# Gate's copy of the logits and its tanh issued one place later, with the steps behind them, in all batches but the last

## The chip, the cores and the metric

The kernel runs on one core of a Trainium2 chip. The metric is the time of one execution on the device, in microseconds. The core's engines are TensorE (PE, with its weight loads shown apart as PEld), VectorE (DVE), ScalarE (ACT), GpSimd (POOL) and SyncE (SP, which here only issues DMAs). Each works through its own instructions in order and waits where an operand or a buffer is not there yet.

## What is computed

Attention with a capped score, then a mixture of experts with one expert per token. The sizes are 8 batches, 12 heads, 448 tokens, head width 64; 3584 tokens of width 768 go to 8 experts of inner width 1024, each of which keeps at most 80 tokens.

```python
scores = cap * np.tanh(np.matmul(q, k.transpose(0, 1, 3, 2)) / sqrt(64) / cap)
attn = softmax(scores)                       # over the last axis
x = (attn @ v).transpose(0, 2, 1, 3).reshape(3584, 768)
logits = x @ w_gate
expert_idx = np.argmax(logits, axis=1)
gate_w = softmax(logits)[np.arange(N), expert_idx]
# per expert: of its tokens the `capacity` ones with the largest gate_w
out[tok_idx] = gate_w[tok_idx, None] * (relu(x[tok_idx] @ w1[e]) @ w2[e])
```

## The kernel before

**Attention.** Two heads make a step `t`, 48 in all, six per batch. `qk` (L1019, L1026) multiplies keys by queries into a PSUM tile `sc` (two buffers), and ScalarE writes tanh of it to `e` (L1027). `expo` (L1032) takes the exp in place. `av` (L1043) multiplies `e` by the values. The softmax sums go POOL (`esum`, L1051 and L1053, into `t`), VectorE (`erem`, L1061, up to step 33), TensorE (`sums`, `sp`, L1068 and L1070), VectorE (`st`, `rc`, `r`). `scaled` (L1085) and `turned` (L1093) make `x` and its transpose `xb`.

**Order.** The order of everything is written out by hand; the instructions stand on each engine as the Python issues them. An even step runs `q0 q1 y m a0 a1 b q2 q3 s b x a2 a3 r b u`, an odd one `q0 q1 y a0 a1 b q2 q3 u n b x a2 a3 b`. Here q is qk with its tanh, x and y the two halves of the exp, a is av, s and r the two erem of the even step, u the sums (odd steps), n and m scaled and turned. Each `b` is a place: three in a step, numbered 0 to 2 in the text. At a place `background` issues work from three lists: `urgent` (the gate), `low` (gathers for the first experts) and `bg` (ranks of tokens, and the expert order). An entry is (cost in ns, function, gap): it is issued only if at least `gap` places have passed since the last entry of its list, and while the place's quota lasts. The quota is the cost still listed, shared out over the places left in the batch, at least 600 and at most 2200 (3000 from step 33 on); an entry may overdraw it once. From step 33 on an estimate of VectorE's backlog holds entries back as well.

**The gate** of a batch is put on `urgent` by `m` of the step in which the batch's last `x` is made (step 8 for batch 0, then every six). Its steps before: `product` multiplies `x` by the gate weights into `lgp` (twelve matmuls, L1112) and ScalarE copies the result to `lgs` (L1119); `turn` transposes it on TensorE into `lt` (L1126); `choice` on VectorE sums, takes the maximum and the differences `d` (L293 to L295), ScalarE takes tanh of half of `d` into `tau` (L296), VectorE finds the chosen expert (L297 to L301); `key` makes the sort key from `tau` (L304 to L312); `later` makes the gate weight and stores it (L317 to L322, the store on SP's queue) and puts the batch's rank steps on `bg`.

**Ranks** (L387 to L421): a row of keys is spread by TensorE (`psk`) and copied by ScalarE (`krow`), VectorE compares (`gb` of up to 896 columns, L408, and `gl`, L395), TensorE counts (`pd`, L415), VectorE adds (`dfc`, L421). Batch 4's are mixed with the steps that order the experts (`pr...`). The tiles `lgp`, `lt`, `sp`, `psk` and `pd` share two PSUM buffers.

**Experts.** Eight weight tiles are loaded ahead from step 39; after step 49 the expert products (L758) run, with what is left of the lists between them.

Of the kernel before, what the change touches and what calls it, by code (L numbers as in the profile page):

```python
# [7 lines left out]
F32 = mybir.dt.float32  # L8
# [3 lines left out]
AF = mybir.ActivationFunctionType  # L12
# [5 lines left out]
B, H, S, D = 8, 12, 448, 64  # L18
# [6 lines left out]
NC = S // C  # L25
# [4 lines left out]
E = 8  # L30
# [6 lines left out]
OB = 5  # L37
# [76 lines left out]
def attn_moe(ctx, tc, q2, k, v, cap, wg, w1, w2, capacity, ct, out):  # L114
    nc = tc.nc
# [152 lines left out]
        nc.tensor.matmul(psn[:, 0:E], ones[:C, :], hs, start=True, stop=True)  # L268
        copy(dst, psn[:, 0:E])

    def gate_math(sm, lt, b, kcb, ohb, gdst, usb=None, cmb=None, ohvb=None, queue=nc.sync):

        sh = [C, NC, E]
        lg = sm.tile(sh, F32, name=f"lg{b}", tag="lg")
        mx = sm.tile([C, NC], F32, name=f"mx{b}", tag="mx")
        d = sm.tile(sh, F32, name=f"d{b}", tag="d")
        tau = sm.tile(sh, F32, name=f"tau{b}", tag="tau")
        cand = sm.tile(sh, F32, name=f"cand{b}", tag="cand")
        cm = sm.tile([C, NC], F32, name=f"cm{b}", tag="cm") if cmb is None else cmb
        pw = sm.tile(sh, F32, name=f"pw{b}", tag="pw")  # L280
        wsc = sm.tile([C, NC], F32, name=f"wsc{b}", tag="wsc")
        rd = sm.tile(sh, F32, name=f"rd{b}", tag="rd")
        w = sm.tile(sh, F32, name=f"w{b}", tag="w")
        u = sm.tile([C, NC], F32, name=f"u{b}", tag="u")

        def up(a):
            return a.rearrange("p (c a) -> p c a", a=1).broadcast_to(sh)

        def row(key):
            return cst(key, C).rearrange("p (a e) -> p a e", a=1).broadcast_to(sh)  # L290

        def choice():
            nc.vector.tensor_reduce(lg, lt.rearrange("p c g e -> p c e g"), axis=AX.X, op=ALU.add)  # L293
            nc.vector.tensor_reduce(mx, lg, axis=AX.X, op=ALU.max)
            nc.vector.tensor_tensor(d, up(mx), lg, op=ALU.subtract)  # L295
            nc.scalar.activation(tau, d, AF.Tanh, scale=0.5)  # L296
            nc.vector.scalar_tensor_tensor(cand, d, 0.0, row("rev"), op0=ALU.is_equal, op1=ALU.mult)  # L297
            nc.vector.tensor_reduce(cm, cand, axis=AX.X, op=ALU.max)
            nc.vector.tensor_tensor(ohb, row("rev"), up(cm), op=ALU.is_equal)
            nc.vector.scalar_tensor_tensor(pw, ohb, 1.0, row("pow"), op0=ALU.mult, op1=ALU.mult)  # L300
            nc.vector.tensor_reduce(wsc, pw, axis=AX.X, op=ALU.add)  # L301

        def key():
            nc.vector.tensor_scalar(rd, tau, 1.0, 0.0, op0=ALU.add, op1=ALU.add, accum_out=dump[:C])  # L304
            nc.vector.reciprocal(rd, rd)
            nc.vector.tensor_tensor(w, tau, rd, op=ALU.mult)
            nc.vector.tensor_reduce(u, w, axis=AX.X, op=ALU.add)
            if usb is not None:
                nc.vector.tensor_scalar(usb, u, 2.0 ** -28, None, op0=ALU.max)
            nc.vector.scalar_tensor_tensor(kcb, u, 2.0 ** -28, wsc, op0=ALU.max, op1=ALU.mult)  # L310
            if ohvb is not None:
                nc.vector.tensor_tensor(ohvb, rev[:C].rearrange("p (a e) -> p a e", a=1).broadcast_to(sh), up(cm), op=ALU.is_equal)  # L312
        return choice, key, lambda: gate_weights(sm, sh, tau, rd, b, gdst, queue)

    def gate_weights(sm, sh, tau, rd, b, gdst, queue):
        w2 = sm.tile(sh, F32, name=f"w2{b}", tag="w2")
        nc.vector.scalar_tensor_tensor(w2, tau, 1.0, rd, op0=ALU.subtract, op1=ALU.mult)  # L317
        g = sm.tile([C, NC], F32, name=f"g{b}", tag="g")
        nc.vector.tensor_reduce(g, w2, axis=AX.X, op=ALU.add)
        nc.vector.tensor_scalar(g, g, -1.0, 1e-9, op0=ALU.mult, op1=ALU.add)  # L320
        nc.vector.reciprocal(g, g)
        queue.dma_start(gdst, g)  # L322
# [513 lines left out]
    def attention_rowmax(sm, pl, b):  # L836
# [55 lines left out]
            nc.tensor.transpose(lt[:, c, 0], lg[:, c * C:(c + 1) * C], cst("ident", 32)[:, :32])  # L892
        kcb = sm.tile([C, NC], F32, name="gkc", tag="gkc")
        ohb = sm.tile([C, NC, E], F32, name="goh", tag="goh")
        for f in gate_math(sm, lt[:, :, :, 0:E], "g", kcb, ohb, gdv[:, bass.ds(b * NC, NC)]):
            f()
        nc.sync.dma_start(kcd[:, bass.ds(b * NC, NC)], kcb)
        nc.sync.dma_start(ohd[:, bass.ds(b * NC, NC)], ohb)
# [63 lines left out]
    urgent = []  # L962
# [11 lines left out]
    with ExitStack() as a2:  # L974
# [139 lines left out]
        def gate(b):  # L1114
            def product():
                logits(b, range(NP))
                lp = st["lp", b]
                lg = sm.tile([96, S], F32, name=f"lgs{b}", tag="lgs", bufs=1)
                nc.scalar.copy(lg, lp[0:96, :S])  # L1119
                st["lgs", b] = lg  # L1120

            def turn():
                lg = st["lgs", b]
                lt = ps1.tile([C, NC, 3, 32], F32, name=f"lt{b}", tag="misc", bufs=2)
                for c in range(NC):
                    nc.tensor.transpose(lt[:, c].rearrange("p g e -> p (g e)"), lg[:, c * C:(c + 1) * C], cst("ident", 96)[:, :96])  # L1126
                st["lt", b] = lt

            def math():
                cs = slice(b * NC, (b + 1) * NC)  # L1130
                lt = st["lt", b][:, :, :, 0:E]
                if b < OB:
                    st["math"] = gate_math(sm, lt, b, kc[:, cs], oh[:, cs], gdv[:, cs], us[:, cs], cms[:, cs])
                else:
                    ws = slice(b * NC - OCOL, (b + 1) * NC - OCOL)
                    st["math"] = gate_math(sm, lt, b, kc[:, cs], oh[:, cs], gdv[:, cs], None, cmn[:, ws], ohv[:, ws], nc.sync if b < B - 1 else nc.gpsimd)
            def end(pd):
                r = st["rank"] = consts.tile([C, RCOL], F32, name="rank")
                nc.vector.tensor_tensor(osd, osd, dfc2, op=ALU.add)
                nc.vector.tensor_reduce(r, acc2, axis=AX.X, op=ALU.add)  # L1140
                nc.vector.tensor_tensor(r, r, osd, op=ALU.subtract)
                n = pd.shape[-1]
                nc.vector.tensor_tensor(r[:, :n], r[:, :n], pd, op=ALU.subtract)
                st["chain"]()
            def later():
                st["math"][2]()
                if b < OB:
                    steps = list(ranks(krow, gp, ps1, "misc", b, acc, dfc, 0, 0, []))
                else:
                    steps = list(ranks(krow, gp, ps1, "misc", b, acc2, dfc2, CAND, OCOL, [e * SL for e in range(E)]))  # L1150
                if b == OB - 1:
                    kept = list(prune(krow, gp, ps1, "misc"))
                    n = next(i for i, x in enumerate(kept) if x[0] == 1750)
                    steps = [steps[0], kept[0], *steps[1:4], kept[1], *steps[4:7], kept[2], *steps[7:9], *kept[3:n], *steps[9:], *kept[n:]]
                if b > OB:
                    bg.insert(0, steps.pop(0))
                bg.extend(steps)
                now[2] = now[0]
                ready_at[2] = clock[1]

            def finish():
                st["math"][2]()
                steps = list(ranks(krow, gp, ps1, "misc", b, acc2, dfc2, CAND, OCOL, [e * SL for e in range(E)], end=end))
                f0, f1, f2, f6, f3, f4, f5, f8 = final_order(sm, lambda: ps1.tile([128, 512], F32, name="pcn", tag="misc", bufs=2))
                parts = [(50, lambda i=i, h=h: stored(nc.gpsimd, b, i, slice(NB // 2 * h, NB // 2 * h + NB // 2)), 1) for i in range(4) for h in range(2)]
                head = [(400, f0, 0), steps[0], (200, f1, 1), steps[1], (200, f2, 1), steps[2], (200, f6, 1), (200, f3, 0), steps[3],
                        steps[4], (300, f4, 1), *steps[5:8], (300, f5, 1), *steps[8:10], (300, f8, 1), *steps[10:]]
                n = 4
                for x in parts:
                    head.insert(n, x)  # L1170
                    n += 2
                bg.extend(head)
            st["wait"]()
            urgent.append((300, product, 0 if b < OB else 1))
            urgent.append((300, turn, 1 if b < OB else 2))
            if b < OB - 1:
                urgent.append((2500, lambda: (math(), st["math"][0](), st["math"][1](), later()), 1))
                return
            urgent.append((1900, lambda: (math(), st["math"][0]()), 1 if b < OB else "ordered"))
            urgent.append((1900, lambda: st["math"][1](), 0))  # L1180
            urgent.append((1000, finish if b == B - 1 else later, 0))

        now = [0, -9, -9, -9]
# [240 lines left out]
```

## Time and profile before

| | us |
|---|---|
| median of 3 runs | 524.43 (523.38 to 525.9) |
| profiled execution: time | 523.92 |
| profiled execution: span, first to last instruction | 522.1 |
| TensorE busy in the span | 477.3 (91%) |
| VectorE busy | 344.2 (66%) |
| ScalarE busy | 328.6 (63%) |
| POOL busy | 257.4 (49%) |

Attention takes the span to about 400 us, the experts the rest. A busy share is a mean over both. In a row of the trace, what stands in brackets is the time for which the engine was idle just before the instruction, and who released it.

### The profile page before, as it was taken

The page shows a single profiled execution, that of the slowest core. Times are in us where ns is not written, and L with a number is a line of the kernel's source. Part 1 is how long each engine was busy: PE and PEld are TensorE (multiplying, and loading weights), DVE is VectorE, ACT ScalarE, POOL GpSimd, SP SyncE. Part 2 cuts the span into 40 slices and gives each one's busy share as a digit, 9 for nine tenths or more (in the row PEclk, how much of TensorE's full clock was granted, in tenths as well). Part 3 has the DMA queues.
Part 4 walks back from the last instruction along what each step waited for, and adds up shares of the span by engine and source line. Part 5 has one row for each costly group of instructions (what it writes and reads, how often), then busy time and mean ns, then how long its engine had stood idle before and what let it go on. Part 6 is the DMA issues. An engine that isn't in the chain of part 4 may idle for free. (4 is left out here: it accounts for less than half of the span.)

```text
span 522.1 us, 13512 instructions
## 1 busy us (share of the span) xinstructions
PE 477.3 (91%) x5476; PEld 218.7 (42%) x5476; DVE 344.2 (66%) x783; ACT 328.6 (63%) x326; POOL 257.4 (49%) x175
## 2 busy tenths in 40 slices
PE   6899999999899999999999998989999978887894
PEld 2223322332332323333323332233335778787894
DVE  1177789878988998899889866984669624512000
ACT  4998879788787978788777875857890101011111
POOL 0666657554664645576356443635964064043001
PEclk9999999999999999999999999989999998999999
DMA  6655359667765774578538769783659789999931
GB/s 165 184 167 148 92 105 222 173 187 87 199 212 131 105 231 108 94 143 251 131 87 163 166 157 257 120 216 106 196 109 315 239 220 407 381 383 398 361 127 45
DMA packets 74103, 99.03 MB, mean 190 GB/s; under 512 B 16976, under 2 KB 59248, under 8 KB 74032
## 3 DMA queue, kind: packets, MB, share of 16 engines
q1 hardware_dynamic: 72048, 93.45, 65.8%
q0 software_dynamic: 1984, 4.63, 2.8%
q8 instruction: 45, 0.74, 0.6%
q14 instruction: 26, 0.21, 0.2%
HBM read 74.54 MB, written 23.51 MB: 188 GB/s over the span
## 5 line engine op out<-in xcount | busy, mean ns | idle before, releaser
L1027 ACT ACTIVATE e<-sc,scl 128x896 f32<-128x896 f32 x168 | 162.4, 1005 | 55.0 <-PE sc L1019 53.0
L1043 PE MATMUL av<-e,vr 128*32 128x448 f32 x1536 | 174.3, 546 | 3.7 <-ACT e L1032 1.9
L1053 POOL TENSOR_TENSOR t<-t,e 128x896 f32<-128x896 f32 x48 | 109.4, 2279 | 92.6 <-ACT e L1032 85.6
L1032 ACT ACTIVATE e<-e,capt 128x1792 f32<-128x1792 f32 x96 | 153.6, 1601 | 0.0
L1019 PE MATMUL sc<-qt,kt 64*128 64x448 f32 x576 | 139.1, 585 | 12.5 <-ACT e L1027 7.5
L1051 POOL TENSOR_TENSOR t<-e 128x896 f32<-128x896 f32 x48 | 106.1, 2211 | 74.9 <-ACT e L1032 74.9
L1061 DVE SCALAR_TENSOR_TENSOR t<-t,e 64x448 f32<-64x448 f32 x68 | 93.0, 1378 | 29.7 <-ACT e L1032 28.5
L1043 PEld LDWEIGHTS av<-e,vr 128*32 128x32 f32 x1536 | 46.7, 109 | 100.8 <-issue 72.1
L1019 PEld LDWEIGHTS sc<-qt,kt 64*128 64x128 f32 x576 | 49.7, 191 | 89.8 <-issue 41.7
L408 DVE TENSOR_SCALAR_CACHE_REDUCE gb<-krow,kc 112x896 bf16<-112x896 f32 (+16 forms) x59 | 53.9, 930 | 8.0 <-ACT krow L388 4.4
L758 PE MATMUL yt<-thv,w 128*64 128x80 f32 x1152 | 44.5, 235 | 10.1 <-issue 10.1
L758 PE MATMUL hp<-xt,w 128*64 128x80 f32 x1152 | 44.7, 237 | 2.4 <-issue 2.4
L758 PEld LDWEIGHTS yt<-thv,w 128*64 128x64 f32 x1152 | 41.9, 137 | 12.0 <-issue 12.0
L758 PEld LDWEIGHTS hp<-xt,w 128*64 128x64 f32 x1152 | 42.5, 140 | 5.1 <-issue 4.8
L1073 DVE STREAM_TRANSPOSE st<-sp 128x448 f32<-128x448 f32 x24 | 15.5, 647 | 34.1 <-PE sp L1070 18.6
L802 POOL DMA_INDIRECT out_dram<-ysv,si x6 | 5.7, 956 | 56.0 <-ACT ysv L801 37.4
L1093 DVE STREAM_TRANSPOSE xb<-x 128x448 f32<-128x448 f32 x48 | 30.8, 644 | 1.6
L1068 PE MATMUL sp<-t,ones 128*32 128x448 f32 x192 | 28.2, 551 | 3.4 <-DVE t L1061 2.0
L774 ACT COPY ty0v<-yt 128x240 f32<-128x240 f32 x6 | 2.1, 358 | 46.1 <-PE yt L758 46.1
L1085 DVE TENSOR_TENSOR x<-av,r 128x448 f32<-128x448 f32 x48 | 29.5, 616 | 0.8
L1026 PE MATMUL sc<-qt,kt 64*64 64x448 f32 x192 | 23.6, 562 | 0.0
L774 DVE COPY ty1v<-yt 128x240 f32<-128x240 f32 x1 | 0.4, 408 | 33.8 <-ACT ty0v L774 33.8
(216 smaller groups left out, 302.9 us busy)
## 6 DMA issues: line engine op xcount, KB each, us to landing
w<-in_w_dram SPq DMA_DIRECT2D x36, 512.0 KB, 8.2
w<-in_w_dram SPq DMA_DIRECT2D x48, 384.0 KB, 6.0
kt<-in_k_dram SPq DMA_DIRECT2D x96, 112.0 KB, 3.6
qt<-in_q_dram SPq DMA_DIRECT2D x96, 112.0 KB, 2.8
xs<-xb SPq DMA_DIRECT2D x28, 336.0 KB, 5.9
vr<-in_v_dram SPq DMA_DIRECT2D x24, 256.0 KB, 3.6
out_dram<-zero SPq DMA_DIRECT2D x4, 1536.0 KB, 7.2
vr<-in_v_dram SPq DMA_DIRECT2D x24, 192.0 KB, 3.0
```

What stands on the lines that cost most here:

```text
L408: nc.vector.tensor_scalar(g, krow[:, x:y], kp, 0.0, op0=ALU.is_ge, op1=ALU.add, accum_out=a)
L758: nc.tensor.matmul(ps[j // per][64 * h:64 * h + 64, j % per * m:(j % per + 1) * m], w[:, 128 * j + 64 * h:128 * j + 64 * h + 64], x[:, kk, ...
L1019: nc.tensor.matmul(ps[:, h, :S], s["k"][w, x:x + CK], s["q"][w], start=True, stop=True)
L1027: nc.scalar.activation(s["e"][:, 2 * c:2 * c + 2], ps[:, :, :S], AF.Tanh, scale=scl)
L1032: nc.scalar.activation(x, x, AF.Exp, scale=capt)
L1043: nc.tensor.matmul(st["av", u, f][32 * g:32 * g + 32, :S], st[p]["v"][:, g % 2, c, 32 * f:32 * f + 32], late(p) if c == NK else st[p]["e"] ...
L1051: nc.gpsimd.tensor_tensor(t1, e[:, 0:2], e[:, 2:4], op=ALU.add)
L1053: nc.gpsimd.tensor_tensor(s["es"], s["es"], e[:, 4:6], op=ALU.add)
L1061: nc.vector.scalar_tensor_tensor(t1[w, h], t1[w, h], 0.0, late(p)[w], op0=ALU.add, op1=ALU.add)
L1068: nc.tensor.matmul(sp[32 * g:32 * g + 32, :S], ones[:, 0:32], s["es"][:, g % 2, :], start=True, stop=2 * u < RMB)
L1085: nc.vector.tensor_tensor(x, st["av", u, f][:, :S], st["r", u], op=ALU.mult)
L1093: nc.vector.transpose(st["xt", b][:, :, j, :], st["x", b, j].rearrange("p (a b) -> p a b", b=32))
```

## The change

In all batches but the last the copy of the logits is no longer issued with the product but as an entry of its own with gap 1 (`kept`), and the tanh no longer inside `choice` but as an entry with gap 1 between `choice` and `key` (`half_angle`). `turn`, `choice`, `key` and `later` come in later places by that. In batches 0 to 3, where choice, key and later were one entry of cost 2500, they are entries of their own. The last batch keeps its order. No instruction is added or taken away.

```diff
-    def gate_math(sm, lt, b, kcb, ohb, gdst, usb=None, cmb=None, ohvb=None, queue=nc.sync):
+    def gate_math(sm, lt, b, kcb, ohb, gdst, usb=None, cmb=None, ohvb=None, queue=nc.sync, now_=True):
...
+        def half_angle():
+            nc.scalar.activation(tau, d, AF.Tanh, scale=0.5)
+
         def choice():
...
             nc.vector.tensor_tensor(d, up(mx), lg, op=ALU.subtract)
-            nc.scalar.activation(tau, d, AF.Tanh, scale=0.5)
+            if now_:
+                half_angle()
...
-        return choice, key, lambda: gate_weights(sm, sh, tau, rd, b, gdst, queue)
+        return choice, key, lambda: gate_weights(sm, sh, tau, rd, b, gdst, queue), half_angle
...
             def product():
                 logits(b, range(NP))
-                lp = st["lp", b]
-                lg = sm.tile([96, S], F32, name=f"lgs{b}", tag="lgs", bufs=1)
-                nc.scalar.copy(lg, lp[0:96, :S])
-                st["lgs", b] = lg
+                st["lgs", b] = sm.tile([96, S], F32, name=f"lgs{b}", tag="lgs", bufs=1)
+                if b == B - 1:
+                    kept()
+
+            def kept():
+                nc.scalar.copy(st["lgs", b], st["lp", b][0:96, :S])
...
             urgent.append((300, product, 0 if b < OB else 1))
-            urgent.append((300, turn, 1 if b < OB else 2))
-            if b < OB - 1:
-                urgent.append((2500, lambda: (math(), st["math"][0](), st["math"][1](), later()), 1))
-                return
+            if b < B - 1:
+                urgent.append((100, kept, 1))
+            urgent.append((300, turn, 1 if b < B - 1 else 2))
             urgent.append((1900, lambda: (math(), st["math"][0]()), 1 if b < OB else "ordered"))
-            urgent.append((1900, lambda: st["math"][1](), 0))
+            if b < B - 1:
+                urgent.append((100, lambda: st["math"][3](), 1))
+                urgent.append((1900, lambda: st["math"][1](), 1))
+            else:
+                urgent.append((1900, lambda: st["math"][1](), 0))
             urgent.append((1000, finish if b == B - 1 else later, 0))
```

## Rows read from the trace of the kernel before

**Rows 1.** Busy time by engine in a quiet period (columns in the first line).
```profile
core 0: us, PE busy (x) PEld busy (x) DVE busy (x) ACT busy (x) POOL busy (x), PEclk, DMA share, GB/s
33.82:47.84 14.02, 14.02 (x106) 4.34 (x104) 10.32 (x14) 12.63 (x11) 9.54 (x5) 1.00 0.66 189
```

**Rows 2.** ScalarE's waits, 60 to 375 us: total, times, longest.
```profile
ACT e L1027 <- PE sc L1019: 42.8, 47, 4.3
ACT tau L296 <- DVE d L295: 17.2, 6, 4.6
ACT lgs L1119 <- PE lgp L1112: 2.0, 7, 0.4
```

**Rows 3.** Timeline of TensorE: start, duration, [idle before]; three like 264.84's.
```profile
73.25 1.02 PE L1019 MATMUL sc<-qt,kt 64*128 64x448 f32 x4 [1.23 <-ACT e L1027]
120.42 1.02 PE L1019 MATMUL sc<-qt,kt 64*128 64x448 f32 x4 [0.97 <-ACT e L1027]
264.84 1.02 PE L1019 MATMUL sc<-qt,kt 64*128 64x448 f32 x4 [0.98 <-ACT e L1027]
323.00 1.70 PE L1043 MATMUL av<-e,vr 128*32 128x448 f32 x12 [1.87 <-ACT e L1032]
```

**Rows 4.** Timeline of all engines around the gate of batch 0.
```profile
65.70 0.53 ACT L1119 COPY lgs<-lgp 96x448 f32<-96x448 f32 x1 [0.26 <-PE lgp L1112]
67.52 1.78 ACT L1032 ACTIVATE e<-e,capt 128x1792 f32<-128x1792 f32 x1
69.38 2.37 POOL L1051 TENSOR_TENSOR t<-e 128x896 f32<-128x896 f32 x1 [1.26 <-ACT e L1032]
69.72 0.24 DVE L293 TENSOR_REDUCE lg<-lt 112x32 f32<-112x96 f32 x1
70.22 1.58 DVE L295 TENSOR_TENSOR d<-mx,lg 112x32 f32<-112x32 f32 x1
71.83 0.23 ACT L296 ACTIVATE tau<-d 112x32 f32<-112x32 f32 x1 [2.53 <-DVE d L295]
74.69 0.18 DVE L321 RECIPROCAL g<-g 112x4 f32<-112x4 f32 x1
```

**Rows 5.** Timeline, the gate of batch 6.
```profile
370.50 0.19 DVE L295 TENSOR_TENSOR d<-mx,lg 112x32 f32<-112x32 f32 x1
370.72 0.23 ACT L296 ACTIVATE tau<-d 112x32 f32<-112x32 f32 x1
```

**Rows 6.** Groups of instructions by shape, ScalarE: busy us, mean ns, idle before.
```profile
L1027 ACT ACTIVATE e<-sc,scl 128x896 f32<-128x896 f32 x168 | 162.4, 1005 | 55.0 <-PE sc L1019 53.0 <-POOL t L1053 1.6
L1032 ACT ACTIVATE e<-e,capt 128x896 f32<-128x896 f32 x24 | 25.0, 1040 | 0.0
```

**Rows 7.** Timeline of VectorE and TensorE after batch 5's gate.
```profile
317.19 0.65 DVE L1073 STREAM_TRANSPOSE st<-sp 128x448 f32<-128x448 f32 x1 [7.28 <-PE sp L1070]
339.37 1.81 PE L1043 MATMUL av<-e,vr 128*32 128x448 f32 x16 [1.13 <-DVE x L1085]
344.04 1.03 PE L565 MATMUL prt<-prrh,prlh 112*96 112x40 bf16 x20 [1.91 <-DVE prrh L559]
```

**Rows 8.** Timeline of TensorE: its waits for VectorE ahead of the sums.
```profile
91.46 0.94 PE L1068 MATMUL sp<-t,ones 128*32 128x448 f32 x2 [0.60 <-DVE t L1061]
138.66 0.96 PE L1068 MATMUL sp<-t,ones 128*32 128x448 f32 x8 [1.42 <-DVE dfc L421]
186.37 0.56 PE L1068 MATMUL sp<-t,ones 128*32 128x448 f32 x1 [0.98 <-DVE t L1061]
249.06 1.21 PE L1068 MATMUL sp<-t,ones 128*32 128x448 f32 x3 [0.15 <-DVE t L1061]
```

**Rows 9.** Groups of instructions by shape, VectorE's rank steps.
```profile
L408 DVE TENSOR_SCALAR_CACHE_REDUCE gb<-krow,kc 112x896 bf16<-112x896 f32 x25 | 28.0, 1132 | 0.1
L395 DVE SCALAR_TENSOR_TENSOR gl<-krow,kc,ctt 112x112 bf16<-112x112 f32 x32 | 22.6, 707 | 0.0
L421 DVE TENSOR_TENSOR dfc<-dfc,pd 112x14 f32<-112x14 f32 x2 | 0.3, 144 | 0.0
```

**Rows 10.** Busy time by engine and granted clock (columns as in rows 1).
```profile
212.00:262.00 50.00, 48.87 (x398) 16.68 (x394) 45.09 (x91) 39.89 (x37) 27.79 (x13) 1.00 0.68 153
346.04:349.45 3.41, 3.41 (x14) 1.19 (x8) 3.22 (x11) 0.26 (x1) 0.99 (x1) 0.50 0.99 232
71.50:77.00 5.50, 4.27 (x40) 1.26 (x36) 3.69 (x19) 5.03 (x7) 2.08 (x2) 1.00 0.19 15
```

More of the change, by code (lines that the diff above doesn't have):

```diff
@@ L894, in attention_rowmax @@
         ohb = sm.tile([C, NC, E], F32, name="goh", tag="goh")
-        for f in gate_math(sm, lt[:, :, :, 0:E], "g", kcb, ohb, gdv[:, bass.ds(b * NC, NC)]):
+        for f in gate_math(sm, lt[:, :, :, 0:E], "g", kcb, ohb, gdv[:, bass.ds(b * NC, NC)])[:3]:
             f()
@@ L1132, in math @@
                 if b < OB:
-                    st["math"] = gate_math(sm, lt, b, kc[:, cs], oh[:, cs], gdv[:, cs], us[:, cs], cms[:, cs])
+                    st["math"] = gate_math(sm, lt, b, kc[:, cs], oh[:, cs], gdv[:, cs], us[:, cs], cms[:, cs], now_=False)
                 else:
                     ws = slice(b * NC - OCOL, (b + 1) * NC - OCOL)
-                    st["math"] = gate_math(sm, lt, b, kc[:, cs], oh[:, cs], gdv[:, cs], None, cmn[:, ws], ohv[:, ws], nc.sync if b < B - 1 else nc.gpsimd)
+                    st["math"] = gate_math(sm, lt, b, kc[:, cs], oh[:, cs], gdv[:, cs], None, cmn[:, ws], ohv[:, ws], nc.sync if b < B - 1 else nc.gpsimd, b == B - 1)
             def end(pd):
```

## The prediction

> **What bounds the kernel now.** I read the stretches by engine first, then who waits for whom, then the gaps on TensorE in order of time, and last the order of all engines around one gate.
>
> In two steps (a period) before the first gate, TensorE is busy for all of 14.02 us while ScalarE is busy 12.63 and VectorE 10.32 [rows 1]. So in the attention stage TensorE sets the pace, ScalarE has 1.39 us to spare in a period and VectorE 3.70.
>
> ScalarE's waits from 60 to 375 us [rows 2]: 42.8 us are for scores of TensorE, which is what a follower looks like. 17.2 us, in six pieces, are the gate's tanh waiting for VectorE's subtraction `d`. The copy of the logits waits only 2.0 us in seven pieces. So of the two instructions moved, the tanh matters and the copy does not, unless such a wait reaches TensorE.
>
> The tanh's wait does. On TensorE six gaps end with ScalarE's `e` [rows 3]: 1.23, 0.97, 0.98, 0.98, 0.98 us just after the gates of batches 0 to 4, where a score product has no free PSUM until ScalarE's tanh has read an older one, and 1.87 us after batch 5, where `av` waits for an exp. Sum 7.01. The first gate [rows 4]: ScalarE ends its exp at 67.52 + 1.78 = 69.30; `d` starts at 70.22 and takes 1.58 because POOL's sum, 69.38 to 71.75, overlaps it (where no POOL sum overlaps it takes 0.19, [rows 5]); the tanh starts at 71.83, having waited 2.53, with two score tanhs behind it. TensorE resumes at 73.25 [rows 3]. In batch 6 the tanh follows `d` at once, with no idle time before it on ScalarE [rows 5]; batch 7 is unchanged.
>
> **Part by part.** A step has three places; in even steps the first follows a0 a1, the second the q2 q3 and s, the third x, a2 a3 and r; in odd steps the second follows u and n.
>
> *The tanh, batches 0 to 4.* Following gaps and costs through the planner by hand, batch 0 runs product, turn, choice+tanh+key in step 8's places 0, 1, 2 before. After: product, copy, turn there, choice in step 9's place 0, tanh in place 1, key in place 2, weights in step 10's place 0. Batches 1 to 4 repeat this. VectorE has nothing between the erem of `r` in step 8 and choice, so choice still starts at about 69.7 and `d` still ends at about 71.8. ScalarE now has q0, q1, y, q2, q3 ahead of its tanh: 4 x 1.00 plus 1.04 us of work [rows 6], so it gets there at 69.30 + 5.04 = 74.3 at the earliest. It no longer waits: `d` has been ready for over 2 us. ScalarE then reads the scores in time, and each gap closes: 1.23 + 0.97 + 3 x 0.98 = **5.1 us**. Bounds: 0 (if something else is late at that point) and 5.1. I take 5.1, because these gaps have one releaser, and everything else that the score product needs is old by then.
>
> *The tanh, batch 5.* The planner puts turn and choice where they were and the tanh two places after choice (the place between has other work but does not let the tanh go). Its wait, the longest of [rows 2] at 4.6 us, goes. But VectorE has no pause from 317.19, when `sp` releases it after 7.28 us of idleness, past 344.04 [rows 7]. Twice in that stretch TensorE waits for it: 1.13 us for `x`, 1.91 us for `prrh`. The change only reorders VectorE's work in there (key and weights behind the rank steps). What TensorE gains at 323, it waits at 339: **0 us**, bounds -0.5 and 1.87.
>
> *The copy.* Before, it ran in a gap (0.26 us of waiting, 0.53 of work, [rows 4]) in which ScalarE had no scores yet. After, it stands behind q2's tanh and ahead of x's exp, so exp ends 0.5 us later. The 1.39 us spare hides it. Without that cover it would cost 7 x 0.53 = 3.7. I take 0. `turn` then follows a2 a3 instead of preceding them; the copy has ended by then. Between product and copy no other tile takes the logits' PSUM buffer (two buffers, shared with sums, keys and counts): where a count is issued in between (batches 3 and 4) it takes the other buffer, and the older count's `add` stands ahead.
>
> *Key, weights and rank steps, later.* No instruction is added. Choice, key and weights took 69.72 to 74.87 = 5.15 us in one piece, in VectorE's lull ahead of `sp` [rows 4]. After, choice (about 3.1 us) stays in that lull, and key and weights, about 2.0 us, move into the next two steps. The rank steps of batches 0 to 3 start three to four places later, and their larger remaining cost raises the quota, so more stand in one period. What matters is VectorE's work between one `st` and the erem that the next `sp` needs. In the first period after a gate the rank work was 3.7 to 4.8 us, and TensorE waited 0.60, 1.42, 0.98 and 0 us for batches 0 to 3 [rows 8]; in the second it was about 2 to 5.6, with one wait for `t`, 0.15 us in batch 3 [rows 8]. After, the first period has 2.0 us, so its 3.0 us of waits go. The second, by the durations of [rows 9] (0.71 per `gl`, 1.13 per `gb` of 896, others in proportion, 0.14 per `add`), has 3.2, 3.5, 5.8 and 4.7 us for batches 0 to 3; batch 2's, say, is `gb` 0.29 + 1.13 + 0.44 + 1.13 + 0.55, three `gl` and an `add`. VectorE's spare time was 3.70 in a quiet period; TensorE's own rank and gate products lengthen the period by about 1. So 4.7 us are hidden, or little less, and the overflow is about 0, 0.3, 1.2 and 0.4, with one more instruction caught behind POOL (1.4 us, as `d` was) perhaps 0.6 more: 2.5 in all. Net **0.5 us gained**; bounds: 3.2 gained (all waits of [rows 8] gone, none new) and 3.5 lost (an overflow of 6.5).
>
> *Queues.* SP's store of the weights `gd` goes four places later. It waits for VectorE's `g` at the head of SP's queue; behind it stand loads of q and k for three steps ahead, some 21 us of cover against at most 2 to 3 us of waiting: 0. On POOL one gather of batch 6's stretch goes two places earlier, behind the transposes that free its buffer: 0, bounds -1 and 1. Everything from step 48 on is issued in the same places as before, so the expert stage shifts as a whole: 0.
>
> **Sum.** On the profiled execution: 523.92 (span 522.1, 1.8 around it) - 5.1 - 0.5 = 518.3. The median of the runs is 524.43, 0.5 above that execution, so the forecast is 524.4 - 5.6 = **518.8 us**.
>
> **Rivals.**
>
> A, more is returned: batch 5's 1.87 us stays and the waits of [rows 8] go without successors: 5.1 + 1.9 + 3.2 = 10.2, so 514.2; one half of that surplus makes 516.5. For it: the first period becomes light. Against: VectorE's unbroken stretch of [rows 7].
>
> B, VectorE's pile-up takes half: the second periods overflow by 6.5 us, so 5.1 - 3.5 = 1.6 gained, 522.8. For it: VectorE was busy 45 of 50 us at 212 to 262 us [rows 10]. Against: 5.6 us of rank work in such a period cost only 0.15 [rows 8].
>
> C, slower: the same pile-up, and TensorE's clock. After the idle 1.91 us before 344.04 the granted clock fell to 0.50 (1.2 GHz) for 3.41 us [rows 7, 10], which costs 1.7 us of work; after the gate's gap of 1.23 it stayed at 1.00 (2.4 GHz, [rows 10]). If batches 1 to 3 each leave TensorE idle 2.7 us in a second period and each draws such a stretch, that is 3 x (2.7 + 1.7) = 13.2 lost, less 5.1 and 3.0 gained: 529.5. It decides against the change from 10.7 us of new losses on. Against: an overflow of 2.7 needs 7.4 us of rank work in a period, in three batches.
>
> D, nothing: ScalarE, not TensorE, sets the pace, so that gaps closed on TensorE open elsewhere: 524.4. For it: ScalarE is busy 12.63 of 14.02. Against: in the quiet period ScalarE waits for scores and TensorE for nothing [rows 1, 2]. The Trainium skill (Perfetto Trace Analysis, Identifying the Most-Contended Engine) says that the busy share of matmuls is a poor measure of how near TensorE is to its limit, and to look at weight loads instead; those are 4.34 of 14.02 here, so by that rule D would hold. The waits speak for TensorE all the same.
>
> **How the numbers follow.** Forecast 0.50 (517 to 520.6 us), A 0.14 (514.2 to 517), B 0.22 (520.6 to 524), C 0.07, D 0.07. The range 515.0 to 523.5 leaves out C, D and the far ends of A and B, about 0.2. A measurement of this kernel can tell about 0.5%, 2.6 us, from no change, so faster means below 521.8: forecast, A and a little over half of B, 0.76. Within 0.5%: the rest of B and D, 0.17. Slower: C, 0.07.
>
> **What would show it.** In the changed kernel's trace the six waits of tanh for `d` are gone or below 0.5 us, and TensorE has no gap that ends with `e` after the gates of batches 0 to 4. The rounds of those five batches are each about 1 us shorter. At 335 to 345 us the waits for `x` and `prrh` have grown by the 1.9 us of batch 5. TensorE's waits for `t` before `sp` move from the first to the second period after a gate and sum to about 2.5 us. I am wrong if tanh still waits (choice late), if those second periods show gaps of 2 us or more, or if the stage after 390 us is not a shifted copy.

## The result, and the profile after

The changed kernel takes 518.18 us (median of 6 runs, 515.55 to 525.18) against 524.29 for the kernel before beside it: ratio 0.985, 95% interval 0.981 to 0.990. The ratio leaves out the one slow run, 525.18; the two medians by themselves give 0.988. Two later measurements gave 0.988 (0.980 to 0.996) and 0.993 (0.989 to 0.997). The forecast was 518.8. The profiled execution took 516.19 us, with a span of 514.3 against 522.1 before. Line numbers moved by three to seven: L1027 of before is L1031 after, L295 is L298, L421 is L425, L1068 is L1072, L1119 (the copy) is L1126. L296 (the tanh) is L293.

ScalarE's waits from 60 to 375 us (total, times, longest), the answer to [rows 2]:
```profile
ACT e L1031 <- PE sc L1023: 48.2, 53, 4.5
ACT e L1031 <- issue: 4.5, 4, 2.0
ACT e L1031 <- POOL t L1055: 2.2, 1, 2.2
ACT krow L585 <- PE prk L584: 1.5, 2, 1.1
```
The tanh's row (17.2 us) is gone, and so is the copy's. Around batch 0's gate, the answer to [rows 4] (start, duration):
```profile
66.46 0.52 ACT L1126 COPY lgs<-lgp 96x448 f32<-96x448 f32 x1
69.16 1.73 DVE L298 TENSOR_TENSOR d<-mx,lg 112x32 f32<-112x32 f32 x1
73.84 0.22 ACT L293 ACTIVATE tau<-d 112x32 f32<-112x32 f32 x1
```
`d` ends at 70.89 and the tanh starts at 73.84 with no idle time before it. Now TensorE's waits from 60 to 305 us, first of before, then of after:
```profile
PE sc L1019 <- ACT e L1027: 5.1, 5, 1.2
PE sp L1068 <- DVE t L1061: 2.0, 4, 1.0
PE sp L1068 <- DVE dfc L421: 1.4, 1, 1.4
```
```profile
PE lt L1132 <- DVE dfc L425: 2.6, 2, 1.6
PE pd L419 <- DMA vr<-in_v_dram: 1.9, 1, 1.9
PE sp L1072 <- DVE dfc L425: 1.7, 1, 1.7
PE sp L1072 <- DVE t L1065: 0.2, 1, 0.2
```
The gates' gaps of 5.1 us [rows 3] are closed and the waits of [rows 8] are nearly gone, but new ones of 6.2 us stand in their place. (The one put down to a DMA is a wait for VectorE's `gb`, which two later traces of the change name: it starts at 183.12, 1.5 us after the product before it, and `pd` runs 0.06 us after it ends.)

The way from batch 0's gate logits to batch 5's, in before and after (columns as in [rows 1]; the window is the first):
```profile
63.94:305.96 242.02, 232.41 (x1831) 76.45 (x1825) 210.26 (x425) 195.87 (x182) 135.70 (x60) 1.00 0.67 154
62.88:298.79 235.91, 229.11 (x1832) 76.52 (x1825) 205.07 (x420) 196.25 (x182) 129.83 (x60) 1.00 0.68 157
```
These "five rounds" hold the same work of TensorE and are the sharpest measure of this case: in a second trace of before they took 242.02 again. The span's 7.8 us divide so: the start up to batch 0's logits 1.06, the five rounds 6.11, from there to the first expert product 1.87, and the expert stage gave 1.23 back. Only the 6.11 are plainly the change's. Nothing that it moves stands ahead of batch 0's logits, and these start at 62.7 to 63.9 us in the fourteen traces of this case; the stretch behind the five rounds took 85.69 and 87.74 in two traces of before and 83.82, 85.73 and 85.42 in three of the change.

### The profile page after: what moved, and what is told of

It reads as the page before. It is cut to its first block, busy times and chain, and to the rows that moved or that the text cites. A ratio compares the mean times of both kernels' runs of the same rounds, so it can differ in the third digit from the quotient of the medians.

```text
span 514.3 us, 13524 instructions
## 1 busy us (share of the span) xinstructions
PE 471.8 (92%) x5476; PEld 216.8 (42%) x5476; DVE 339.3 (66%) x783; ACT 328.7 (64%) x326; POOL 251.8 (49%) x175
## 5 line engine op out<-in xcount | busy, mean ns | idle before, releaser
L1031 ACT ACTIVATE e<-sc,scl 128x896 f32<-128x896 f32 x168 | 162.9, 1006 | 64.6 <-PE sc L1023 55.9
L1057 POOL TENSOR_TENSOR t<-t,e 128x896 f32<-128x896 f32 x48 | 106.2, 2213 | 91.1 <-ACT e L1036 80.0
L1055 POOL TENSOR_TENSOR t<-e 128x896 f32<-128x896 f32 x48 | 103.4, 2155 | 73.0 <-ACT e L1036 73.0
L762 PEld LDWEIGHTS hp<-xt,w 128*64 128x64 f32 x1152 | 41.3, 137 | 7.0 <-issue 6.8
L1072 PE MATMUL sp<-t,ones 128*32 128x448 f32 x192 | 24.1, 551 | 1.9 <-DVE dfc L425 1.7
L772 ACT ACTIVATE thv<-hp 128x640 f32<-128x640 f32 x6 | 4.2, 704 | 29.2 <-PE hp L762 29.2
```

Source lines behind the costliest of these rows:

```text
L762: nc.tensor.matmul(ps[j // per][64 * h:64 * h + 64, j % per * m:(j % per + 1) * m], w[:, 128 * j + 64 * h:128 * j + 64 * h + 64], x[:, kk, ...
L1031: nc.scalar.activation(s["e"][:, 2 * c:2 * c + 2], ps[:, :, :S], AF.Tanh, scale=scl)
L1055: nc.gpsimd.tensor_tensor(t1, e[:, 0:2], e[:, 2:4], op=ALU.add)
L1057: nc.gpsimd.tensor_tensor(s["es"], s["es"], e[:, 4:6], op=ALU.add)
L1072: nc.tensor.matmul(sp[32 * g:32 * g + 32, :S], ones[:, 0:32], s["es"][:, g % 2, :], start=True, stop=2 * u < RMB)
```

## Experiments

"Five rounds" is the window above. "Attention's end" is the first expert product `hp`, "expert stage" from there to the last instruction. Ratios are to before in the same runs.

**The tanh alone, the copy where it was.** Against the changed kernel:
```
-                if b == B - 1:
-                    kept()
+                kept()                      # in product, all batches
...
-            if b < B - 1:
-                urgent.append((100, kept, 1))
-            urgent.append((300, turn, 1 if b < B - 1 else 2))
+            urgent.append((300, turn, 1 if b < OB else 2))
```


> The tanh and the steps behind it one place later as in the change, the copy of the logits back in the product's place. Theory 1 (the tanh's wait for d is what TensorE paid for; the later copy gives nothing and, by way of the transposes lt, which waited 1.60 and 0.96 us for an add in batches 3 and 4 of the changed kernel, costs about 2.5 us): no wait of tanh for d, no gap of lt, 1.0 to 2.5 us faster than the changed kernel, so 513 to 517 us, span of the profile 511 to 514. Theory 2 (the later copy is part of the gain, because ScalarE reads q2's scores before it): tanh's waits gone but at most 4 us faster than the kernel before, 520 or more.


Ratio 0.984 (0.973 to 0.994). Five rounds in 228.55 us: 13.5 less than before, where the whole change gave 6.1. No wait of the tanh, none of `lt`. From batch 5's logits to attention's end it takes 87.54 us (85.69 and 87.74 in two traces of before). The first theory holds, but its price was too small: the five rounds are 7.4 us shorter than the change's, where it had 1.0 to 2.5. The total doesn't show that (0.984 against the change's 0.985), since the expert stage took 140.23 us here.

**The copy alone, one place later, the tanh inside choice.** Against before:
```
+            def kept():
+                nc.scalar.copy(st["lgs", b], st["lp", b][0:96, :S])
...
-            urgent.append((300, turn, 1 if b < OB else 2))
+            if b < B - 1:
+                urgent.append((100, kept, 1))
+            urgent.append((300, turn, 1 if b < B - 1 else 2))
```


> Only the copy of the logits goes one place later, and turn, choice with the tanh, key and weights follow it together; the tanh is not taken out of choice. Theory 1 (what counts is only how much of ScalarE's own work stands between its exp and the tanh, while d ends at the same time as before because VectorE is held by the erem until then): in batches 0 to 4 tanh reaches ScalarE's head after q0, q1 and y, about 3 us later than before, so its wait falls from 2.5 us to under 0.5 and TensorE's five gaps of 1 us close: 3 to 6 us faster, 518 to 521 us. Batch 5's wait of 4.6 us stays, since turn stands where it was. Theory 2 (the split of tanh from choice is what does it): the six waits stay at 2.5 us and the time within 1.5 us of before, 523 to 526.


Ratio 0.988 (0.982 to 0.993), five rounds 236.59. Only two waits of a tanh are left (4.5 us in batch 5 and one of 2.2), none in batches 0 to 4, and TensorE has no gap behind those gates. In batch 0 the copy is at 66.75 and the tanh at 71.72, still inside choice. So the gates' gaps close when either of the two comes later; the tanh need not leave choice.

**The change without batches 5 and 6.**
```
-            if b < B - 1:                   # copy, turn, tanh
+            if b < OB:
```


> The change in batches 0 to 4, batches 5 and 6 as before. Theory 1 (batch 5's wait was worth 2.6 us in the changed kernel, since the stretch from st of step 39 to st of step 41 took 17.00 us there and 19.59 before): 2 to 3 us slower than the changed kernel, 519 to 521 us, with the wait of 4.5 us and TensorE's gap of 1.9 us back after batch 5. Theory 2 (as predicted: VectorE's unbroken stretch gives that gain back, and the 2.6 us came from elsewhere): the same stretch of about 17 us, time as the changed kernel, 516 to 518.


Ratio 0.991 (0.986 to 0.996). Five rounds 235.91, the changed kernel's to 0.01. Batch 5's tanh waits 4.5 us again and `av` 1.87. From VectorE's `st` of step 39 to that of step 41 it takes 19.49 us, as in before (19.59); in the changed kernel 17.00. These 2.5 us don't reach attention's end, though: from batch 5's logits to there it takes 83.07 us, against 83.82 in the changed kernel. The total decides between the theories as little (the change itself had 0.985 to 0.993).

**The tanh with key and weights in one place.** Against the first experiment, batches 0 to 3 (in batches 4 to 6 key may follow in the tanh's place, too):
```
+                urgent.append((1500, lambda: (math(), st["math"][0]()), 1))
+                urgent.append((1000, lambda: (st["math"][3](), st["math"][1](), later()), 1))
```


> The copy where it was; the tanh one place after choice, and key and weights in the tanh's own place. Theory 1 (one place of distance is enough for the tanh, and every further place only pushes the rank steps together): tanh's waits below 0.5 us in batches 0 to 4, VectorE waits at most 0.5 us for tau, TensorE's waits for t and dfc before sp sum to less than in the changed kernel: 512 to 516 us. Theory 2 (key needs its own later place, because VectorE reaches it before ScalarE has done tau behind q0, q1 and y): VectorE idle 0.5 to 2 us before rd in each batch, and sp later by that: 518 to 522 us.


Ratio 1.003 (0.998 to 1.008), five rounds 237.25. No tanh waits, so its 5 us come back, but `sp` waits 2.6 us for `t` in five pieces. The other 8.7 us of the first experiment came only where key and weights have places of their own (the costs entered here, 1500 and 1000, are another difference). Behind the five rounds it loses: 89.81 us to attention's end. Both theories had expected it to be faster than before.

**Before once more**, on another chip, beside the next three.


> The kernel before, unchanged, for a trace of it on the chip that runs the three beside it, since the four edits tried so far all lost time in the expert stage against a trace of before from another chip (the attention of the tanh-only edit ended 12.8 us earlier and its last instruction 3.0 us earlier). If the loss belongs to the edits, this trace's expert stage, from the first hp matmul to the end, takes the 130.5 us of the first trace. If it belongs to the chip or to stretches at half clock, it takes some 4 to 10 us more here.


Span 526.5: five rounds 242.02, expert stage 133.16 against 130.48 in the first trace, between what the two cases had.

**The changed kernel again.**


> The changed kernel, unchanged, beside the tanh-only edits on one chip. Theory 1: moving the copy and what follows it costs 6 us of attention (waits of 2.6 us of the counts' loads, 1.7 and 1.9 us of TensorE for the counts' adds), so that the last gate logits start 7 to 8 us earlier than in before and no more. Expected ratio to before 0.985, the same as measured first. Theory 2, that the kernel's gain depends on the chip: a ratio over 0.993.


Ratio 0.988, as the first theory had it. Five rounds 237.23, the steps of batch 5 19.50 us (17.00 in the first trace): two differences that are taken up below.

**The tanh alone, batches 0 to 4**, all else as before, but choice, key and weights with places of their own as in the change.
```
+            if b < OB:
+                urgent.append((100, lambda: st["math"][3](), 1))
+                urgent.append((1900, lambda: st["math"][1](), 1))
+            else:
+                urgent.append((1900, lambda: st["math"][1](), 0))
```


> Only the tanh and its readers one place later, only batches 0 to 4; copy and batches 5 and 6 as before. Theory 1 (the copy's move costs 6 us of attention, and the batches behind the tail of attention give nothing by the move): no wait of a tanh in batches 0 to 4, no wait of the counts' loads for VectorE's dfc add, start of batch 5's logits about 14 us earlier than in before (14.6 in the tanh-only edit), batch 5's stretch about 19.5 us, hp0 12 to 15 us earlier; ratio 0.975 to 0.983, below the changed kernel's. Theory 2 (the gain of attention is given back behind it whatever is done, since the expert stage runs against its weight loads): hp0 12 us earlier, but the end 3 to 8 us earlier; ratio 0.984 to 0.992.


513.03 us, ratio 0.980 (0.973 to 0.987). The first theory holds: five rounds 228.51, attention's end 15.6 us earlier than in before on that chip, the last instruction 18.2. The tanh's waits that are left, 4.8 us in two pieces, lie behind batch 4. Where the 13.5 us come from, by groups in the five rounds (busy us, mean ns | idle before), before first:
```profile
L1043 PE MATMUL av<-e,vr 128*32 128x448 f32 x964 | 108.2, 544 | 0.7 <-DVE x L1085 0.7
L1068 PE MATMUL sp<-t,ones 128*32 128x448 f32 x120 | 19.4, 551 | 3.4 <-DVE t L1061 2.0 <-DVE dfc L421 1.4
L1061 DVE SCALAR_TENSOR_TENSOR t<-t,e 64x448 f32<-64x448 f32 x56 | 74.7, 1342 | 14.2 <-ACT e L1032 13.2
```
```profile
L1047 PE MATMUL av<-e,vr 128*32 128x448 f32 x964 | 103.5, 544 | 3.0 <-DVE x L1089 3.0
L1072 PE MATMUL sp<-t,ones 128*32 128x448 f32 x120 | 14.4, 551 | 0.0
L1065 DVE SCALAR_TENSOR_TENSOR t<-t,e 64x448 f32<-64x448 f32 x56 | 65.4, 1180 | 8.7 <-ACT e L1036 7.8
```
Its five rounds as a whole:
```profile
63.49:292.00 228.51, 224.67 (x1832) 74.58 (x1825) 200.96 (x423) 197.07 (x182) 133.94 (x61) 1.00 0.71 163
```
TensorE's idle time fell by 242.02 - 232.41 - (228.51 - 224.67) = 5.8 us; the other 7.7 came out of its *busy* time, with as many products of the same mean length. About half of that is in `sp`, half in `av` (5.0 and 4.7 us by the rows, which overlap). The 120 `sp` need 14.4 us end to end when their operands are there; in before they show 19.4, because they start one by one as VectorE's `t` arrives (the last row of [rows 8] has three in 1.21 us), and the run counts as busy. With `av` it is ScalarE's exp that comes late inside a run: seven runs of 16 products in before take 0.2 to 0.5 us longer than the others, none here by more than 0.1. The first of them in before, and the same run here:
```profile
81.12 1.79 ACT L1032 ACTIVATE e<-e,capt 128x1792 f32<-128x1792 f32 x1
82.47 2.19 PE L1043 MATMUL av<-e,vr 128*32 128x448 f32 x16
```
```profile
78.72 1.79 ACT L1036 ACTIVATE e<-e,capt 128x1792 f32<-128x1792 f32 x1
80.59 1.71 PE L1047 MATMUL av<-e,vr 128*32 128x448 f32 x16
```
In before the run starts 0.44 us ahead of the exp's end, here 0.08 behind it. VectorE's 56 `t` products took 9.3 us less. One with no POOL sum beside it takes 0.62 and the longest 2.53; 24 of the 56 took over 1 us in before, 19 here, so fewer were held by one of POOL's sums.

**`d` by four instructions with one tensor input each**, in the kernel before.
```
-            nc.vector.tensor_tensor(d, up(mx), lg, op=ALU.subtract)
-            nc.scalar.activation(tau, d, AF.Tanh, scale=0.5)
+            for c in range(NC):
+                nc.vector.tensor_scalar(d[:, c], lg[:, c], mx[:, c:c + 1], 0.0, op0=ALU.subtract, op1=ALU.add, accum_out=dump[:C])
+            nc.scalar.activation(tau, d, AF.Tanh, scale=-0.5)
```


> The kernel before, with d made by four instructions that have only one tensor input each, so that none of them shares a port with a running sum of GpSimd if that is what makes d 1.58 us in place of 0.19. Theory 1 (d is long because GpSimd holds what its second tensor input needs; the tanh's wait comes from it): the four d take under 0.3 us each also beside a GpSimd sum, the tanhs of batches 0 to 4 wait 1 to 1.7 us in place of 2.5 to 2.7, TensorE's gaps behind them (1.23 to 0.97 us) fall to 0 to 0.4, batch 5's tanh wait falls from 4.6 by about 2 or less; 2 to 5 us faster. Theory 2 (VectorE is late with d for its place in its queue, not for the port): tanh waits over 2.2 us and gaps over 0.8 us as before, no more than 1 us faster. Theory 3: any instruction of VectorE waits for GpSimd there, and the first of the four takes over 1 us.


Ratio 0.993 (0.989 to 0.997). Batch 0's gate:
```profile
68.22 2.37 POOL L1052 TENSOR_TENSOR t<-e 128x896 f32<-128x896 f32 x1 [1.26 <-ACT e L1033]
69.06 0.22 DVE L296 TENSOR_SCALAR_CACHE_REDUCE d<-lg,mx 112x8 f32<-112x8 f32 x1
69.85 0.22 DVE L296 TENSOR_SCALAR_CACHE_REDUCE d<-lg,mx 112x8 f32<-112x8 f32 x1
70.11 0.23 ACT L297 ACTIVATE tau<-d 112x32 f32<-112x32 f32 x1 [1.97 <-DVE d L296]
71.54 1.02 PE L1020 MATMUL sc<-qt,kt 64*128 64x448 f32 x4 [0.67 <-ACT e L1028]
```
Inside the same sum the four take 1.0 us together, where one with two inputs took 1.58, and the tanh starts at 70.11, while the sum runs to 70.59. The five gaps fall from 5.1 to 2.4 us and the five rounds from 242.02 to 239.29: 2.7, all of what the gaps lost. It is the first theory's mechanism, but smaller than it had it: the wait is 1.97 in place of 1 to 1.7 us, the gaps up to 0.67 in place of 0.4, since `lg` and `mx` alone bring the tanh late. Batch 5's gap grew (1.87 to 2.70 us): no sum runs beside its `d` (0.19 us in before), and there the four only take longer.

**`d` issued later**: its `mx` found five times over, in before.
```
+            for _ in range(5):
                 nc.vector.tensor_reduce(mx, lg, axis=AX.X, op=ALU.max)
```


> The kernel before, with the greatest logit of each token found five times in place of once, so that d is issued 0.75 to 0.9 us later in every gate. Theory 1 (in batches 0 to 4 a running sum of GpSimd holds d until it ends; the tanh's start is the sum's end): d starts 0.8 us later and takes about 0.8 us in place of 1.58, the tanhs of batches 0 to 4 start within 0.3 us of where they did against the logits' copy, TensorE's gaps behind them keep 0.9 to 1.3 us; batch 6, where no sum runs beside d, has its tanh 0.8 us later. Theory 2 (d takes 1.58 us whenever it is issued beside a sum): tanh and gap both 0.8 us later in batches 0 to 4, gaps 1.7 to 2.1 us.


Batch 0 of before (its second trace), then of this kernel:
```profile
68.97 2.37 POOL L1051 TENSOR_TENSOR t<-e 128x896 f32<-128x896 f32 x1 [1.26 <-ACT e L1032]
69.81 1.58 DVE L295 TENSOR_TENSOR d<-mx,lg 112x32 f32<-112x32 f32 x1
71.42 0.23 ACT L296 ACTIVATE tau<-d 112x32 f32<-112x32 f32 x1 [2.52 <-DVE d L295]
```
```profile
69.04 2.38 POOL L1052 TENSOR_TENSOR t<-e 128x896 f32<-128x896 f32 x1 [1.26 <-ACT e L1033]
70.76 0.70 DVE L296 TENSOR_TENSOR d<-mx,lg 112x32 f32<-112x32 f32 x1
71.50 0.23 ACT L297 ACTIVATE tau<-d 112x32 f32<-112x32 f32 x1 [2.53 <-DVE d L296]
```
Against the sum's start `d` starts 0.88 us later, and it ends where it did, 0.05 and 0.04 us behind the end of the sum (71.34 and 71.42). In all five batches the tanh's wait is 2.52 or 2.53. The five rounds take 242.35 us. So the first theory holds: the sum's end sets the tanh's start, not VectorE's place. The Trainium skill (SBUF — State Buffer, the section on its two separate sides) says that an instruction of VectorE with two inputs in SBUF and a GpSimd one that reads SBUF lock each other out for a whole instruction. These rows agree: 1.58 and 0.70 under the sum, 0.19 without one [rows 5], 0.22 under it with one input.

**The changed kernel, the tanh alone to batch 4, and to batch 5, side by side.** The last against the second:
```
-            if b < OB:
+            if b < OB + 1:
```


> The changed kernel once more, as the measure for the two tanh-only edits beside it on one chip. Expected ratio to before 0.985 to 0.990.

> Only the tanh and its readers later, batches 0 to 4, a second time and with more executions. Theory 1 (the copy's move costs some 6 us of attention and some 8 us by the first hp): ratio 0.975 to 0.983, at least 4 us below the changed kernel. Theory 2 (the lead of the first trace came from that chip): within 2 us of the changed kernel.

> As the tanh-only edit of batches 0 to 4, and batch 5's tanh and its readers later too; batch 6 as before. Theory 1 (in the changed kernel batch 5's move gave back 2.6 us, with the copy moved; without the copy's move it gives the same): no wait of batch 5's tanh (4.6 us in the edit of batches 0 to 4), the gap of 1.9 us on TensorE gone, st18 to st19 in 17 us in place of 19.6, 2 to 3 us faster than the edit of batches 0 to 4; ratio 0.970 to 0.978. Theory 2 (the edit of all batches to 6 lost 2.5 us between the logits of batch 6 and its end because batch 5's steps came later, not because of batch 6's): st18 to st19 in 17 to 19.6 us and st20 to st21 2 us longer than in the edit of batches 0 to 4; ratio as that edit's.


Ratios 0.993 (0.989 to 0.997), 0.978 (0.974 to 0.982) and 0.977 (0.973 to 0.981); five rounds 235.90, 228.50, 228.47. (The change had been expected at 0.985 to 0.990.) The tanh alone to batch 4 is faster than before and than the change beside it, and its interval doesn't meet the change's.

The third edit doesn't move batch 5's tanh. It adds the entry, but the call of `gate_math` for batch 5 still leaves the tanh inside `choice`, so that ScalarE runs it twice:
```profile
307.11 0.23 ACT L293 ACTIVATE tau<-d 112x32 f32<-112x32 f32 x1 [4.55 <-DVE d L298]
312.38 0.22 ACT L293 ACTIVATE tau<-d 112x32 f32<-112x32 f32 x1
```
The wait of 4.55 us is still there, `av` still waits 1.31 us, and steps 39 to 41 take 19.33 us (19.58 without the entry, where I had expected 17). So this kernel decides neither of its theories. What batch 5's tanh does with the copy in its place is seen in the first experiment: the wait for `d` is gone, and TensorE waits 3.68 us for `x` in place of 1.12. From batch 5's logits to batch 6's it takes 54.94 us there, with 6.8 of them at half clock, against 55.45 and 55.40 with the tanh alone to batch 4, with 3.4 at half clock.

## Why the prediction was right, and where it was not

**The tanh, batches 0 to 4: 5.1 us.** Right in size and reason. `sc` has no wait left, and the tanh is reached 2.95 us after `d` ended. The two experiments on `d` show what had made it wait: POOL's sum. Batch 6 has no such wait in [rows 5], but that is one execution's: in the second trace of before its `d` met a sum, took 2.27 us, and the tanh waited 4.23.

The five rounds became shorter by 2.4, 0.7, 1.9, 0.2 and 1.0 us, not by about 1 each.

**The sum: luck, in good part.** The tanh and its readers alone are worth 13.5 us where the sum had 5.6 (8.7 of them came only with places of their own for key and weights), and the copy costs 7.4 where it had nothing. The two errors nearly cancel.

**Key, weights and rank steps: net 0.5 us (3.0 gone, 2.5 new).** In the changed kernel the net was near, by errors that cancel. Measured over the five rounds: gates 5.1 gone, the other waits of before 4.5 gone (9.61 idle in all), new idle 6.80, and 3.30 out of busy time (232.41 to 229.11) that no wait row showed. 5.1 + 4.5 + 3.3 - 6.8 = 6.1, where I had 5.1 + 3.0 - 2.5 = 5.6. The step that failed is that I took TensorE's rows of waits for all that it waits. The Trainium skill (Perfetto Trace Analysis, Optimization Strategy) says to find the gaps on the engine that one optimizes for. The tanh-alone kernel shows how far that reaches here: 5.8 us of its 13.5 were gaps.

**The copy: 0.** This was the worst step. In the change it costs 7.4 us: 235.91 with it against 228.51, with all else alike but the places of what follows it (the third experiment against the tanh alone to batch 4). I wrote that a count issued between product and copy "takes the other buffer, and the older count's `add` stands ahead". The `add` stands ahead, but behind products under POOL's sum. Batch 3 of the changed kernel:
```profile
203.18 2.08 POOL L1057 TENSOR_TENSOR t<-t,e 128x896 f32<-128x896 f32 x1 [2.58 <-ACT e L1036]
203.50 4.05 DVE L1065 SCALAR_TENSOR_TENSOR t<-t,e 64x448 f32<-64x448 f32 x4 [1.50 <-ACT e L1036]
207.48 0.15 DVE L425 TENSOR_TENSOR dfc<-dfc,pd 112x11 f32<-112x11 f32 x1
207.77 0.51 PE L1132 MATMUL lt<-ctt,lgs 96*112 96x96 f32 x4 [1.60 <-DVE dfc L425]
```
The gate's `lt` needs the buffer that `dfc` reads; `dfc` stands behind four `t` products, the first of them under the sum; and TensorE waits 1.60 us, 0.96 more in batch 4. With the waits at 148.55 (`sp` for `dfc`, 1.68) and 183.47 (`pd` for `gb`, 1.88) these are 6.1 us, where the tanh alone has 3.8 of idle in all, 3.0 of it for `x`. The rest of the 7.4 lies in busy time (229.10 against 224.67). In the changed kernel:
```profile
L1047 PE MATMUL av<-e,vr 128*32 128x448 f32 x964 | 107.7, 544 | 0.0
L1072 PE MATMUL sp<-t,ones 128*32 128x448 f32 x120 | 15.3, 551 | 1.9 <-DVE dfc L425 1.7 <-DVE t L1065 0.2
```
`sp` is within 0.9 us of the tanh alone (14.4), but `av` takes 107.7 us, 4.2 more than there: nine runs of 16 products again wait inside for an exp. VectorE's 56 `t` take 73.9 us, hardly less than the 74.7 of before, and as many of them, 24, take over 1 us. The copy's half microsecond on ScalarE was hidden, as I said: no wait of TensorE ends with it. What was not is the place of everything that follows the copy.

**Batch 5: 0.** In the change no run speaks against it, and its reason holds in two traces of three. From batch 5's logits to batch 6's it takes 55.47 and 55.46 us in two traces of before, and 52.88, 53.42 and 52.85 in three of the change. These 2 to 2.6 us are not the tanh's: without batches 5 and 6 it takes 52.05, no more. What else shortens this round is not shown. Inside the round, the stretch from 39 to 41 was decided by 0.01 us. It took 17.00, 19.50 and 19.50 us. In the first trace, then in the second:
```profile
319.37 0.18 DVE L508 TENSOR_TENSOR r<-r,os 112x20 f32<-112x20 f32 x1
319.38 2.13 POOL L1055 TENSOR_TENSOR t<-e 128x896 f32<-128x896 f32 x1 [0.46 <-ACT e L1036]
```
```profile
320.98 2.10 POOL L1055 TENSOR_TENSOR t<-e 128x896 f32<-128x896 f32 x1 [0.44 <-ACT e L1036]
320.99 2.12 DVE L508 TENSOR_TENSOR r<-r,os 112x20 f32<-112x20 f32 x1
```
VectorE's `r` starts 0.01 us ahead of the sum and takes 0.18, or 0.01 behind it and takes 2.12 (in the third trace 0.02 behind, and 2.12). Four of VectorE's instructions are held in the stretch where it lost, three where it won. Where it lost, TensorE's wait for `x` was 3.68 us, against 1.13 in before [rows 7]: batch 5's gap was given back there, as the prediction had it. But the next two steps took 16.65 and 16.07 us where it lost and 18.60 where it won, so that the round hardly shows the race. The first trace's time, 516.19, lies in rival A's range, but not by A's reason.

**Queues and the expert stage: 0.** No wait came from a queue. The stage was not a shifted copy: 130.48 us in before, 131.71, 131.36 and 143.96 in three traces of the change. The spread is no effect of the change (below).

**Rivals.** B's pile-up came in part: 4.1 us in second periods (1.7, 1.9, 0.5) where the sum had 2.5. C's fall of the clock came once: in the second trace of the change the clock fell to 0.50 at 183.7 for 3.41 us after the 1.89 us in which TensorE waited for `gb`; the five rounds were 1.3 us longer for it (237.23 against 235.91). In the other two traces the same wait, 1.88 us, was followed by no fall. D fell: closing TensorE's gaps of 5.1 us made the five rounds shorter, so TensorE set the pace there.

**What stays open.** Which of the steps behind the copy costs its 7.4 us was read from the waits of one pair of kernels; none of them was moved by itself while the copy stayed in its later place. Nor is it shown why the exp comes late in those runs of `av`, or what made batch 5's round shorter. It was not tried whether the change with a one-input `d` would lose less.

## What to carry to other kernels

When an engine waits for a short instruction, look at what that instruction met, not only at where it was issued: a 0.2 us subtraction under another engine's 2.4 us sum cost five gaps here. One input fewer halved them (5.1 to 2.4 us), and a reader placed later closed them. Move the reader alone; moving what feeds it shifts everything behind it onto other collisions, and here took back 7.4 of 13.5 us. Cost a move by the time between two marks with equal work in between, since waits inside a run of products count as busy.

## What the runs showed of the hardware

The expert stage took 130.5 to 144.0 us, and traces of one and the same kernel differ as much as kernels do (131.4 to 144.0 for the change). A good part of the difference lies in one place, from the 385th to the 577th of the 1152 `yt` products: 7.5 to 9.4 us in six traces, 14.1 to 15.8 in six others, 12 in two (7.51 and 15.61 for the change). In the six long ones TensorE runs at half clock for part of it, in the six short ones it doesn't. Two stretches of the tanh alone to batch 5, ahead of the fall and after it:
```profile
455.10:458.50 3.40, 1.53 (x31) 1.13 (x29) 0.00 (x0) 0.54 (x1) 1.37 (x2) 1.00 1.01 368
458.50:461.90 3.40, 3.40 (x59) 3.40 (x56) 1.14 (x3) 0.17 (x1) 1.85 (x2) 0.51 1.04 400
```
The DMA engines are busy all the time (1.01, 368 GB/s) and TensorE is busy 1.53 of 3.40 us, in pieces with gaps of 0.4 to 1.1 us between them. In the next stretch it is busy throughout, at 1.2 GHz. I read the pieces as waits for the weights, which no experiment shows, nor why some executions have them. A gain of a few us in the attention of this kernel is safely read from attention's marks, and only from many runs in the total.
